# Decay-delta attention and a conv-gated MoE on one core: block-diagonal state of 120x480, w_out in single fp32 matmuls, three solves on GpSimd, new order

## The chip, the cores and the metric

One core of one Trainium2 chip. The metric is the device time of one execution in microseconds; the median of three runs is compared. fp32 inputs and output; the MoE weights arrive as 64-bit words and are converted on the chip.

## The reference

For batch 4, 8 heads, 768 positions and head size 40, a 40x40 state runs along the sequence; the result, heads side by side, is the x of a gated MLP (320 to 1024 to 320) with a convolution of three taps along the sequence.

```python
for t in range(S):
    y[:, :, t] = np.einsum('bhd,bhde->bhe', rt, state)
    Sa = np.einsum('bhde,bhe->bhd', state, at)
    state_decay = state * wt[:, :, None, :] - np.einsum('bhd,bhe->bhde', Sa, bt)
    state = state_decay + np.einsum('bhd,bhe->bhde', vt, kt)
...
h = np.maximum(x @ w_in, 0.0)
...
    conv_out += conv_w[k][None, None, :] * hp[:, k:k + S, :]
gate = 1.0 / (1.0 + np.exp(-conv_out))
return (h * gate @ w_out).astype(np.float32)
```

## The kernel before

The sequence is cut into 24 steps of 32 positions. Partitions hold 4 batches of 32 positions, or 120 = 3 heads x 40 channels. Two steps make a pair, and the 8 heads are cut into three overlapping groups of three (columns from 0, 120 and 200).

Per pair: w, a, k, b are loaded; `decays` turns w (TensorE transposes) and scans it on VectorE; `decayed` turns and scales a, k, b into ah, kt, bt; `scores` masks ah by head (ScalarE, tile ap) and multiplies it with kt and bt (tile at); `hats` turns kt and bt back (khat, bhat); `solve_in` and `solve` invert a unit triangular 32x32 system for each of 64 (batch, head, step): the data go through DRAM to put one system on a partition, 31 rounds of two tensor_tensor (lines 480 and 486) run on VectorE for even pairs (`VSOL`) and on GpSimd for odd ones, and the result comes back through DRAM as tt.

Per step, `chain`: pp = ah with the state plus at with v; psb (ScalarE); pu = tt with psb; u (ScalarE); pn = khat with v plus bhat with u, the update of the state. The state is four tiles s of 120x360, one a batch: for each group of heads a 120x120 block, of which the three 40x40 blocks on the diagonal are wanted; the rest is zeroed by wc, a decay with a head mask (line 381). VectorE adds pn to the old state (line 562), GpSimd multiplies by wc (568). `rturn`, `turn` turn r, v and u; `sturn` turns the state with 12 transposes and four copies to sn (602, 604); `pairs` and `outputs` form py from r with sn and from masked products with khat and bhat; `finish` turns it, scales it and splits it into an fp32r high part xh and a rest xl.

Two steps make a window of the MoE. `moe_in` (four a window, 256 hidden units each): 8 fp32r matmuls for each 128 hidden units give ph, ReLU to hb (714), three taps to cc (721 on ScalarE, 729 on VectorE), sigmoid (734), the product with h (736), then a split into gh on ScalarE (740) and gl on GpSimd (743). `moe_out` (two a window): for each 128 hidden units gh with woh, gl with woh, gh with wol, 24 fp32r matmuls into po (754). Weights are converted by eight VectorE instructions a piece and split into high and low parts.

PSUM: six banks for the attention, two for ph and po. What each engine does next is written out by hand: the generators above are advanced one stage at a time in the sequence of the table `ORDER`, so each engine's queue follows that table, and so does SP's, which issues every DMA.

Of the kernel before, what the change touches and what calls it, by code (L numbers as in the profile page):

```python
# [8 lines left out]
F32 = mybir.dt.float32  # L9
# [11 lines left out]
VSOL = range(0, 12, 2)  # L21
NWA = 24
BUFS = dict(
    ld=4, r=2, v=2, hat=2, suf=2, pre=3, al=2, wc=3, at=3, ah=3, kt=2, ap=1, rp=1, bb=1, xx=1, stmp=1,
    tt=2, rt=1, s=2, psb=1, u=2, vt=2, sn=4, ms=1, ysb=1, xf=2, xh=2, xl=2, xp=1, hb=2, cc=2, o=2,
)
KINDS = dict(
    we="weights", ro="rows", ld="wakb", lv="v", lr="r", de="decays",
# [11 lines left out]
    st1*2 sc4 we6 so1 we8*4 we9 we10 ch1 lv3 rt1 we9 st1*2 ut1 pa1 lr2 ou1 ha4 ld3*2 we10 so1*3 fi0  # L40
    vt2 we10 fi0 fi1 de3.0 sc4 sc5 we9 we10 sc5 ch1 de3.1 we9 de3.1 ha4 we11 we12 lr3 rt2 fi1 st2*2
    fi1 we11 we12 we11*2 ro0 we13 we12*2 ha5 st2 we13 we14 ha5 ld4 so1 we13 dd3.0*3 dd3.1*3 we14*2
    ch2 si2 so2 ch2 pk0 ut2 so2*2 pa2 vt3 sc6 so2*2 st2 ou2 ch2 ro0 rt3 mi0.0*3 so2*2 mi0.0*2 ch2
    st3*2 we13 mi0.1*2 st3 ld4 so2 ld4 we14 lv4 we15 we16 ch3*2 sc6 sc7 ut3 we15 st3 we15 sc7 fi2*3
    lr4 mi0.0 pa3 mi0.0 ch3 we15 ch3 we16 mi0.0 we17 mi0.1 mi0.2 we17*2 mi0.2 so2 ch4 si3 we16 so3
    ou3 ha6 we16 we18 de4.0 we18 ha6 ha7 st4 fi3*2 we17 we19 de4.0 we18 mi0.1 we19 vt4 st4*3 lv5
    de4.1 ch4 ut4 so3 ch4 dd4.0 rt4 we18 we20 de4.1 we20 mi0.2 so3 we20 pa4 vt5 ch4 ch5 so3 mi0.2
    ch5 fi3 ha7 we19*2 we21*2 ut5 we20 we22*2 ou4 st5*2 mi0.1 st5 lr5 rt5 so3 we22 ld4 ld5 de5.0
    mi0.1 we21 ch5 we22 mi0.3 we21 mi0.0*2 so3 mi0.1*2 mi0.3 pa5 mi0.3 pk1 dd4.0*2 dd4.1 mi0.1*2
    dd4.1 st5 mi0.2 sc8 fi4*2 ld5 dd4.1 ou5 mi0.2 lv6 mi0.3 so3*2 sc8 mi0.2 sc9 mi0.2*2 ha8*2 ha9  # L50
    fi4 fi5 ld5 de5.0 de5.1 ha9 sc9 mi0.2 dd5.0 mi0.3 dd5.0 de5.1 lv7 mi1.0*3 mi1.1 ld5 dd5.0 dd5.1
    sc10 so3 si4 mi0.3 lr6 dd5.1*2 ch5 mi0.3 lr7 mi0.3 mi1.1*2 mi1.0*3 mi1.1 mi1.2 vt6 sc10 mi0.3
    mo0.0 sc11 mi0.3 mi1.1 mi1.0*2 mi1.1 ch6 st6 mi1.2 ch6*2 sc11 mi1.1*2 mo0.0*2 ch6 mo0.0 mo0.1*5
    ld6 ut6 rt6 ch7 mi1.1 so4 ld6 so4*2 pa6 vt7 st6 fi5*2 st6 so4*2 mi1.0 so4 mi1.2 st6 mi1.3 so4
    mi1.2 so4 lv8 ou6 mi1.0 mo1.0 mi1.2 mi1.3*2 st7*2 ch7 ut7 mi1.1 st7*2 rt7 ch7*2 mo1.0 pa7
    mi1.3*2 fi6*2 pk2 lr8 mi1.2*2 ou7 mi1.2 rt8 so4 si5 ch8 st8*2 mi1.2 mi1.3 mi1.2 mi1.3 ch8*2 lv9
    fi6 mi2.0*2 lr9 ld6 ch8 ha10*2 fi7 mi1.3*2 ha11 ld6 de6.0 vt8 lv10 de6.0 dd6.0 fi7 mi2.0 mi1.3
    mi2.1 ch9 mo1.0 mi2.0*2 de6.1 ch9 de6.1 so5*2 mi2.1 so5 mi2.0 ut8 mi2.1*4 mi2.0 mo0.0 mo1.0*2
    mo1.1 ha11 mi2.0 mi2.1 mo1.1 dd6.0 mo1.1 dd6.0 pa8 vt9 mo1.1 mi2.0*2 dd6.1 so5 fi7 st8*2 mi2.1*2
    dd6.1 so5 ou8 rt9 mi2.2 sc12 mi2.2*2 mi2.3*3 ut9 dd6.1 st9 mi2.1 mi2.2 ch9 mi2.2 mi2.3*2 mi2.2*2  # L60
    ld7 de7.0 lr10 ld7*2 so5*3 pa9 ch9 lr11 st9*3 pk3 ld7 mi2.3 mi2.2 mi3.0*2 mi2.3 mi3.0 mi2.3 fi8
    so5 fi8 mi2.2*2 mi2.3 mi3.0 ou9 mi3.1 fi8 sc12 fi9 de7.0 dd7.0 sc13 mo2.0*2 sc13 de7.1*2 mi3.1*2
    rt10 ha12*2 ha13 dd7.0 ha13 dd7.0 mi2.3 mi3.0 dd7.1*3 ch10 mi3.1*2 mi3.0 mi3.1 st10 fi9 mo2.0*2
    mo2.1 ch10*3 mo2.1 mi3.0 st10 mi3.1 st10*2 mi3.0 mi3.1 ut10 si6 so6 mi3.2*2 so6 lv11 vt10 mi3.2
    pa10 vt11 so6 mo1.1 so6 mi3.3 mo2.1 mi3.3 ch11 mo2.0 mo2.1 ld8 mi3.0 lr12 so6 ch11 so6 ou10 rt11
    mi3.3 mi3.1 ut11 pa11 st11*3 ld8 lv12 so6 mi3.2 mi3.3 st11 so6 sc14 ch11 vt12 mi3.1 lr13 sc14
    mi3.0 mo3.0 mi3.2 sc15 mi3.2 ch11 mi3.2 fi9 fi10 mi3.3 fi10*2 ou11 st12 ha14 sc15 mi3.2*2 mi3.3
    pk4 so6 ch12 mi3.2 de8.0 mi4.0*2 mi3.3 fi11*2 mi3.3 ch12*2 mo3.0 mi3.3*2 ch12 mi4.0*2 ut12 si7
# [24 lines left out]
    mo7.0 ch20*2 mi8.1*3 ch20*2 mo8.0*2 ha22 mi8.2*2 mi8.3 mi8.2 so11*2 mi8.2 so11 mi8.3*2 pk9 mi8.2
    so11 ha23 mi8.2 ch21 mi8.2*3 st20*2 mi8.3 so11 vt20 lv22 mi8.3 ut20 rt20 lr21 lr22 pa20 vt21
    st20*2 ou20 rt21 st21 mi8.3*3 mi9.0*2 mi8.3*2 mi9.0*2 ch21*2 so11*2 mo7.1 st21 mi9.1*2 ha23 st21
    mi9.1 mi9.0*2 mi9.2 mi9.0 st21 mi9.0 mo8.0*2 mo8.1 mi9.1 so11 mo8.1 mo8.0 mi9.1*3 mi9.2*3 lr23
    ut21 mi9.1 mo8.1*2 mi9.0*2 mi9.3*2 pa21 vt22 mi9.3 fi20*2 ou21 ch21 fi20 mi9.2 mi9.1*2 rt22
    st22*2 mo9.0 mi9.2*2 so11 fi21*3 ch22 st22*2 mi9.2*2 mo9.0 ch22*2 ut22 mi9.3*3 pk10 mi10.0 lv23
    mi10.0*2 mi9.3*3 mi10.1*2 mi9.2 mo9.0 pa22 ch22 ch23 mi10.1 mi9.3 mi10.0*2 mo8.1 vt23 ch23 mo9.0
    mo9.1 mi10.1 mo9.1*2 mi10.0 mi10.1 mi10.0 ut23 mi10.1 mo9.1 ch23 mi10.0*3 mi10.1*2 mi10.2*6 ou22  # L100
    rt23 st23 mi10.1 mi10.3*2 st23*2 mo9.1 fi22 st23 pa23 mi10.2*2 fi22 mi10.1 mi10.3 mi10.2 fi22
# [11 lines left out]
def tile_decay_delta_attention_then_conv_gate_moe(  # L113
# [200 lines left out]
    def cols(g):  # L314
        return slice(GC[g], GC[g] + GR)

# [686 lines left out]
```

## Time and profile before

| | |
|---|---|
| median of three runs (705.96 to 711.5) | 707.8 us |
| profiled execution: span, first to last instruction | 704.2 us |
| its instructions | 29851 |
| TensorE, VectorE, ScalarE, GpSimd busy | 559.1, 521.5, 360.5, 354.1 us |
| mean granted TensorE clock | 0.903 |
| DMA packets, bytes | 242402, 53.40 MB |

The profiled execution's time is its span and whatever lies around it, which no row shows; the span is 3.6 us below the median. The page gives busy time by engine, the span in 40 slices and the chain that ended last; the answers of the trace give busy time by stage, groups of instructions by line (count, busy us, mean ns, idle time before them), waits, and instructions in order of time (start, length, engine, line, tiles, count). PEld is TensorE's weight load. A busy TensorE counts the pipelined end of each matmul, so a rate is read from starts.

### The profile page before, as it was taken

To read this page: it belongs to the slowest core of one execution; us is meant where nothing else is said; L and a number is where in the kernel's file an instruction comes from. 1 tells how busy PE (TensorE), PEld (TensorE's weight loads), DVE (VectorE), ACT (ScalarE), POOL (GpSimd) and SP (SyncE) were. 2 spreads that over 40 slices of the span, in tenths; PEclk is the share of its full clock that TensorE was granted. 3 is DMA by queue.
4 is the path that set the end of the run, shared out by engine and by line. 5 is a ranking of instruction groups with operands and counts; after the bars stand their busy time and mean duration, and the time that the engine had idled before them with its cause. 6 is when DMAs were issued, how large, how long until landed. Compare 5 with 4: busy or idle time off the path is not lost. (4 is left out here: it accounts for less than half of the span.)

```text
span 704.2 us, 29851 instructions
## 1 busy us (share of the span) xinstructions
PE 559.1 (79%) x13021; PEld 496.7 (71%) x13021; DVE 521.5 (74%) x1169; ACT 360.5 (51%) x884; POOL 354.1 (50%) x582
## 2 busy tenths in 40 slices
PE   4436765678688987988987996899998977899886
PEld 3335654666577876977867885788887876788775
DVE  6699789998988895558884478986869892446561
ACT  3322344354275455655464664477665545566661
POOL 2002884037785236783244883237976048854321
PEclk9756766897899998999999998999999999999998
DMA  8766456348036325444414356524444025021000
GB/s 139 121 117 117 96 111 103 86 103 159 7 61 107 61 49 90 87 78 81 84 29 90 75 95 101 81 61 68 86 69 87 11 65 84 20 50 32 22 29 19
DMA packets 242402, 53.40 MB, mean 76 GB/s; under 512 B 229000, under 2 KB 238112, under 8 KB 242272
## 3 DMA queue, kind: packets, MB, share of 16 engines
q1 hardware_dynamic: 242272, 51.50, 40.2%
q8 instruction: 102, 1.67, 1.0%
q14 instruction: 28, 0.23, 0.1%
HBM read 38.63 MB, written 10.22 MB: 69 GB/s over the span
## 5 line engine op out<-in xcount | busy, mean ns | idle before, releaser
L729 DVE SCALAR_TENSOR_TENSOR cc<-hb,cw,cc 128x256 f32<-128x256 f32 x192 | 107.0, 580 | 28.6 <-ACT cc L721 25.0
L568 POOL TENSOR_TENSOR s<-s,wc 120x360 f32<-120x360 f32 x88 | 75.2, 885 | 66.6 <-DVE s L562 66.6
L480 POOL TENSOR_TENSOR st<-xx,bb 128x126 f32<-128x126 f32 (+22 forms) x186 | 81.0, 436 | 20.8 <-DMA bb<-bd 8.1
L486 POOL TENSOR_TENSOR xx<-xx,st 128x126 f32<-128x126 f32 (+22 forms) x186 | 81.8, 440 | 14.6
L700 PE MATMUL ph<-xh,wih 120*128 120x256 f32 x288 | 56.2, 304 | 12.0 <-ACT hb L714 12.0
L562 DVE TENSOR_TENSOR s<-pn,s 120x360 f32<-120x360 f32 x88 | 40.6, 523 | 28.7 <-PE pn L549 28.7
L736 DVE TENSOR_TENSOR cc<-cc,hb 128x512 f32<-128x512 f32 x48 | 40.9, 859 | 26.2 <-ACT cc L734 26.1
L480 DVE TENSOR_TENSOR st<-xx,bb 128x126 f32<-128x126 f32 (+22 forms) x186 | 53.7, 289 | 7.5 <-DMA bb<-bd 1.7
L486 DVE TENSOR_TENSOR xx<-xx,st 128x126 f32<-128x126 f32 (+22 forms) x186 | 54.4, 292 | 6.4
L700 PEld LDWEIGHTS ph<-xh,wih 120*128 120x128 f32 x288 | 41.4, 193 | 17.0 <-ACT hb L714 13.8
L734 ACT ACTIVATE cc<-cc 128x512 f32<-128x512 f32 x48 | 30.5, 637 | 40.8 <-DVE cc L729 40.8
L667 POOL TENSOR_TENSOR xl<-xf,xh 120x384 fp32r<-120x384 f32 x24 | 26.3, 1095 | 44.8 <-ACT xh L665 44.8
L721 ACT ACTIVATE cc<-hb,cw 128x256 f32<-128x256 f32 x96 | 43.8, 507 | 5.0 <-POOL g21l L743 2.4
L427 ACT ACTIVATE ap<-ah,hmask 120x384 f32<-120x384 f32 (+1 forms) x72 | 36.6, 577 | 18.3 <-DVE ah L391 9.7
L604 ACT COPY sn<-pt 120x360 f32<-120x360 f32 x92 | 39.0, 470 | 10.9 <-PE pt L602 10.4
L602 PE MATMUL pt<-ident,s 120*120 120x120 f32 x276 | 40.7, 281 | 4.0 <-DVE s L562 2.4
L714 ACT ACTIVATE hb<-ph 128x512 f32<-128x512 f32 x48 | 28.8, 601 | 22.3 <-PE ph L700 20.5
L579 ACT ACTIVATE rp<-pr,hmask 120x384 f32<-120x384 f32 x72 | 36.7, 585 | 4.7 <-PE pr L576 4.3
L700 PE MATMUL ph<-xl,wih 120*128 120x256 f32 x192 | 39.0, 285 | 0.0
L533 PE MATMUL pu<-psb,tt 32*32 32x40 f32 x1536 | 22.4, 210 | 18.8 <-ACT psb L527 16.1
L602 PEld LDWEIGHTS pt<-ident,s 120*120 120x120 f32 x276 | 31.6, 144 | 6.1 <-DVE s L562 2.8
L533 PEld LDWEIGHTS pu<-psb,tt 32*32 32x32 f32 x1536 | 18.6, 115 | 23.6 <-ACT psb L527 18.1
(867 smaller groups left out, 1661.8 us busy)
## 6 DMA issues: line engine op xcount, KB each, us to landing
bb<-bd SPq DMA_DIRECT2D x24, 256.0 KB
w<-in_w_dram SPq DMA_DIRECT2D x24, 160.0 KB
a<-in_a_dram SPq DMA_DIRECT2D x24, 160.0 KB
k<-in_k_dram SPq DMA_DIRECT2D x24, 160.0 KB
b<-in_b_dram SPq DMA_DIRECT2D x24, 160.0 KB
r<-in_r_dram SPq DMA_DIRECT2D x96, 40.0 KB
v<-in_v_dram SPq DMA_DIRECT2D x96, 40.0 KB
out_dram<-ob SPq DMA_DIRECT2D x22, 160.0 KB
```

Source lines behind the costliest of these rows:

```text
L480: eng.tensor_tensor(t3, xx[:, 0:nj, i : i + 1].to_broadcast([128, nj, nt]), bb[:, i : i + 1, i + 1 :].to_broadcast([128, nj, nt]), ALU.mult,)
L486: eng.tensor_tensor(xx[:, 0:nj, i + 1 :], xx[:, 0:nj, i + 1 :], t3, ALU.add)
L533: nc.tensor.matmul(pu[quad(bi), hc], tt[quad(bi), c, h, :], psb[quad(bi), hc], start=(h == 0), stop=True, skip_group_check=True,)
L562: nc.vector.tensor_tensor(new, pn[bi][:GR], old[bi], ALU.add)
L568: nc.gpsimd.tensor_tensor(n4, n4, w4, ALU.mult)
L579: nc.scalar.activation(out=rp[:, :, h, :], in_=pr[:GR], func=AF.Copy, scale=hmask[:, h : h + 1])
L602: nc.tensor.transpose(pt[:GR, g, :], old[bi][:, g, :], ident[:GR, :GR])
L604: nc.scalar.copy(sn, pt[:GR])
L700: nc.tensor.matmul(ph[:, j], l[:, fs], x, start=(j == 0 and i == 0), stop=(i == len(passes) - 1), skip_group_check=True,)
L721: nc.scalar.activation(out=cc[:, j], in_=hb[:, j, :, 1 : W + 1], func=AF.Copy, scale=cw[:, 1, f : f + 1],)
L729: nc.vector.scalar_tensor_tensor(out=cc[:, j], in0=hb[:, j, :, x : W + x], scalar=cw[:, x, f : f + 1], in1=cc[:, j], op0=ALU.mult, op1=ALU ...
L736: nc.vector.tensor_tensor(cc, cc, hb[:, :, :, 1 : W + 1], ALU.mult)
```

## The change

- **State.** One tile s of 120x480: for each batch three blocks of 40 columns, where block g holds, on its three times 40 rows, one head each. wc loses its mask. pn is now one matmul for each head and batch with 40 streamed columns and 120 weight columns, cut from khat and bhat that lie in a zero-padded layout of 840 columns (`slots`, `spot`), so that the other two heads' columns are zero. The add runs on 120x120, the decay product is one GpSimd instruction of 120x480, `sturn` is four transposes and one copy.
- pp and py take the masked ap and rp per head, 32 matmuls of 40 columns instead of 12 of 120 or 80; rt goes. Groups of heads no longer overlap (3, 3, 2), padded by memsets.
- **v and r** are copied once into DRAM tensors with the heads in the new order (`reorder`, four blocks), and a step then loads each with one DMA.
- **w_out.** The gate stays fp32 in a tile g, the weights in one fp32 tile wo; 8 fp32 matmuls make a moe_out. The copies gh, gl and the split of w_out go.
- **Solves**: `VSOL` is (0, 4, 8); pairs 2, 6 and 10 move to GpSimd.
- `moe_pack` moves rows with two DMAs instead of three. Buffer counts change; `ORDER` is written anew.

```diff
-VSOL = range(0, 12, 2)
+VSOL = (0, 4, 8)
...
-    ld0 de0.0*2 ld0*2 de0.1 ld0 ld1 de0.1 we0 dd0.0*3 dd0.1*2 sc0 dd0.1 we0 ld1*2 lr0 sc0 sc1 lr1
+    ld0 de0.0 ld0*2 de0.0*2 ld0 dd0.0 de0.1*2 ld0 re0 dd0.0 we0 dd0.0 dd0.1 we1 dd0.1*2 dd0.0 sc0
...
+            hat[nm, i] = cp.tile([128, G * PG], F32, name=f"hat{nm}{i}")
+            nc.vector.memset(hat[nm, i], 0.0)
...
+                    nc.sync.dma_start(
+                        ordered[nm, z][bi, :, 3 * h * D : (3 * h + NH[h]) * D].rearrange(
+                            "t (g d) -> t g d", d=D
+                        ),
+                        x[bi, h::3, t0:t1, :].rearrange("g t d -> t g d"),
+                    )
...
-        pn = [bank([128, G, GR], f"pn{n}{bi}") for bi in range(B)]
-        for x, (l, m) in enumerate(((kk, vv), (bk, uu))):
-            for g in range(G):
+        pn = [bank([128, G, D], f"pn{n}{bi}") for bi in range(B)]
+        for x, (l, m) in enumerate(((st["k"], vv), (st["b"], uu))):
+            for q, g, h in heads():
+                lo = spot(q) - D * h
                 for bi in range(B):
                     nc.tensor.matmul(
-                        pn[bi][:GR, g, :], l[quad(bi), cols(g)], m[quad(bi), cols(g)],
-                        start=(x == 0 and g == 0), stop=(x == 1), skip_group_check=True,
+                        pn[bi][:GR, g, :], l[quad(bi), lo : lo + GR],
+                        m[quad(bi), at(q)],
+                        start=(x == 0 and q == 0), stop=(x == 1), skip_group_check=True,
                     )
...
-            for n4, w4 in scaled:
-                nc.gpsimd.tensor_tensor(n4, n4, w4, ALU.mult)
+            nc.gpsimd.tensor_tensor(new, new, w4, ALU.mult)
...
+        pt = bank([128, B, GR], f"pt{n}")
         for bi in range(B):
...
+            nc.tensor.transpose(pt[:GR, bi, :], old[:, bi].rearrange("p g d -> p (g d)"), ident[:GR, :GR])
+        sn = st["sn"] = buf(wn, [GR, B, GR], "sn", f"sn{n}")
+        nc.scalar.copy(sn, pt[:GR])
...
-            gh, gl = parts(f)
-            for l, rr in ((gh, woh), (gl, woh), (gh, wol)):
-                nc.tensor.matmul(
-                    po[:rows, :DM], l, rr[:, f, :],
-                    start=(m == 0), stop=(m == 3 * NF - 1),
-                )
-                m += 1
+            nc.tensor.matmul(
+                po[:rows, :DM], part(f), wo[:, f, :], start=(f == 0), stop=(f == NF - 1)
+            )
```

TensorE at the state update of the eleventh step (pu is the solve's product, pn_... the four batches' banks), before and then now:

```order
L533 MATMUL pu_5857<-psb_5815,tt_5491 32x40 x32
L549 MATMUL pn_5892<-v_4780,khat_4737 120x120
L549 MATMUL pn_5893<-v_4780,khat_4737 120x120
L549 MATMUL pn_5894<-v_4780,khat_4737 120x120
L549 MATMUL pn_5895<-v_4780,khat_4737 120x120
```

```order
L616 MATMUL pu_6135<-psb_6076,tt_5925 32x40 x32
L630 MATMUL pn_6173<-v0t,hatk_137 120x40
L630 MATMUL pn_6174<-v0t,hatk_137 120x40
L630 MATMUL pn_6175<-v0t,hatk_137 120x40
L630 MATMUL pn_6176<-v0t,hatk_137 120x40
```

The four pn rows stood three times for v and three for u; now they stand eight times for each, with 40 columns.

GpSimd where its second solve begins (s are the state products, xx and st the solve's tiles, wil a weight's rest), before and then now:

```order
L568 TENSOR_TENSOR s_2360<-s_2360,wc_677 120x360
L568 TENSOR_TENSOR s_2362<-s_2362,wc_677 120x360
L568 TENSOR_TENSOR s_2364<-s_2364,wc_677 120x360
L568 TENSOR_TENSOR s_2366<-s_2366,wc_677 120x360
L710 MEMSET hb_2413 128x8x2
L473 CAST xx_2479<-xini 128x512
```

```order
L307 TENSOR_TENSOR wil<-wi23q,wih 80x256
L644 TENSOR_TENSOR s_1855<-s_1855,wc_262 120x480
L557 CAST xx_2129<-xini 128x512
L564 TENSOR_TENSOR st_0_2131<-xx_2129,bb_1642 128x31
L570 TENSOR_TENSOR xx_2129<-xx_2129,st_0_2131 128x31
L564 TENSOR_TENSOR st_1_2134<-xx_2129,bb_1642 128x30
```

Before, the second solve on this engine is that of pair 3 and begins behind the four products of the fourth step; now it is that of pair 2, which was on VectorE, it begins behind the one product of the third step and runs in one piece ahead of the fourth step's product.

VectorE's first instructions (wx is what `decays` needs zeroed, hatk and hatb the padded tiles), before and then now, its rows up to those of wx:

```order
L197 MEMSET dsuf 120x192
L200 MEMSET dp_105 120x384
L204 MEMSET wx_107 120x384
L204 MEMSET wx_109 120x384
L198 MEMSET dsuf 120x12
```

```order
L246 MEMSET hatk_137 128x840
L246 MEMSET hatb_139 128x840
L231 MEMSET dsuf 120x12
L246 MEMSET hatk_141 128x840
L246 MEMSET hatb_143 128x840
L250 MEMSET wx_145 120x384
L250 MEMSET wx_147 120x384
```

Eight memsets of 840 columns stand ahead of those of wx.

More of the change, by code (lines that the diff above doesn't have):

```diff
@@ L40 @@
[L40 to L44, printed above, removed]
@@ L200, in tile_decay_delta_attention_then_conv_gate_moe, with padded @@
     nc.vector.memset(dp0, 0.0)
+    def padded(name, at, value):
+        t = cp.tile([128, at + D], F32, name=name)
+        nc.gpsimd.memset(t[:, at:], value)
+        return t
+    inb = {nm: padded(f"in{nm}", 2 * HD, 1.0) for nm in "wakb"}
+    tok = {nm: [padded(f"{nm}{i}t", HD, 0.0) for i in range(BUFS[nm])] for nm in "rvu"}
+    ysb = padded("ysb", HD, 0.0)
+    hat = {}
+    for i in range(BUFS["hat"]):
+        for nm in "kb":
+            hat[nm, i] = cp.tile([128, G * PG], F32, name=f"hat{nm}{i}")
+            nc.vector.memset(hat[nm, i], 0.0)
     wxs = []
@@ L208, in tile_decay_delta_attention_then_conv_gate_moe, with from_f64 @@
     wil = cp.tile([GR, G, DF], F32R, name="wil")
-    woh = cp.tile([128, NF, DM], F32R, name="woh")
-    wol = cp.tile([128, NF, DM], F32R, name="wol")
+    wo = cp.tile([128, NF, DM], F32, name="wo")
     cw = cp.tile([128, KW, NF], F32, name="cw")
-    def from_f64(raw, e, t, m):
+    def from_f64(raw, e, t, m, dst=None):
         lo, hi = raw[..., 0], raw[..., 1]
@@ L294, in load @@
             nc.sync.dma_start(raw, w_out[f * 128 : (f + 1) * 128, 0:512])
-        return piece(f"wo{f}", load, woh[:, f, 0:256], wol[:, f, 0:256], 128, (256,))
+        return piece(f"wo{f}", load, wo[:, f, 0:256], None, 128, (256,))
     def rest_piece(q):
@@ L303, in load @@
             nc.sync.dma_start(raw.rearrange("p (f c) -> p f c", f=4), src)
-        return piece(f"wp{q}", load, woh[:, fs, 256:320], wol[:, fs, 256:320], 128, (4, 64))
+        return piece(f"wp{q}", load, wo[:, fs, 256:320], None, 128, (4, 64))
     pieces = [lambda q=q, g=g: in_piece(q, g) for q in range(4) for g in range(G)]
@@ L314, in cols, with heads @@
     def cols(g):
-        return slice(GC[g], GC[g] + GR)
+        return slice(g * GR, (g + 1) * GR)
+    def heads():
+        return ((q, q // 3, q % 3) for q in range(H))
     def load_wakb(pd):
@@ L576, in rturn @@
             nc.tensor.transpose(pr[:GR, g, :], st["r"][:, cols(g)], ident)
[L577 to L578 removed]
+        rp = st["rp"] = buf(wn, [GR, H, BC], "rp", f"rp{n}")
+        for g in range(G):
             nc.scalar.activation(
[L580 removed]
+                out=rp[:, by_rows(g)], in_=pr[:GR, : NH[g]], func=AF.Copy, scale=hmask[:, g : g + 1]
             )
[L582 to L584 removed]
         yield
@@ L854, in tile_decay_delta_attention_then_conv_gate_moe @@
     )
+    for z in range(len(CUT) - 1):
+        put(("reorder", z), lambda z=z: reorder(z))
     for pd in pds:
```

430 lines of the change are left out of this document (227 added, 203 removed).

## The prediction

> **What bounds the kernel now.** I read the page first: no engine is busy all the time (TensorE 79%, VectorE 74% of the span), and the chain that ended last reaches back only 20 us, to the last gate. So an average says nothing, and I cut the span where the last weights are converted and the first windows of the MoE have begun, at 230 us. The view of busy times by stage:
>
> ```profile
> core 0: us, PE busy (x) PEld busy (x) DVE busy (x) ACT busy (x) POOL busy (x), PEclk, DMA share, GB/s
> 0.00:230.00 230.00, 146.82 (x3457) 125.45 (x3460) 199.11 (x486) 93.72 (x222) 107.05 (x198) 0.79 0.55 102
> 230.00:704.00 474.00, 412.28 (x9586) 371.26 (x9572) 322.38 (x685) 266.76 (x662) 247.10 (x384) 0.96 0.35 63
> ...
> 450.00:500.00 50.00, 47.59 (x1136) 43.68 (x1135) 40.36 (x93) 33.48 (x84) 26.89 (x39) 1.00 0.35 67
> 500.00:550.00 50.00, 45.81 (x1124) 40.78 (x1122) 40.62 (x76) 32.09 (x80) 36.45 (x57) 0.97 0.44 77
> ...
> 600.00:650.00 50.00, 45.74 (x1088) 41.54 (x1087) 23.52 (x43) 29.91 (x76) 31.27 (x52) 0.98 0.15 34
> ```
>
> The first 230 us belong to VectorE (199.1 us, 87%) while TensorE works 147. The other 474 us belong to TensorE: 412.3 us (87%), with VectorE at 68%. The three 50 us rows show how dense TensorE can be in this kernel: 47.59, 45.81 and 45.74 of 50, on average 92.8%. What it waits for in the second part (waits of PE from 230 us on):
>
> ```profile
> PE ph L700 <- ACT hb L714: 12.0, 9, 5.4
> PE py L638 <- issue: 6.3, 7, 1.7
> PE pm L411 <- ACT rp L579: 3.9, 3, 3.3
> ...
> PE po L754 <- ACT g112h L740: 2.7, 1, 2.7
> ```
>
> Many small waits, most of them for ScalarE, and none for the state chain itself. So I treat the change as two sums: VectorE work taken from part 1, and TensorE work added to part 2.
>
> **Part 1, VectorE.** Durations, from the groups by line:
>
> ```profile
> L486 POOL TENSOR_TENSOR xx<-xx,st 128x126 f32<-128x126 f32 (+22 forms) x186 | 81.8, 440 | 14.6
> L480 POOL TENSOR_TENSOR st<-xx,bb 128x126 f32<-128x126 f32 (+22 forms) x186 | 81.0, 436 | 20.8 <-DMA bb<-bd 8.1
> L568 POOL TENSOR_TENSOR s<-s,wc 120x360 f32<-120x360 f32 x88 | 75.2, 885 | 66.6 <-DVE s L562 66.6
> L486 DVE TENSOR_TENSOR xx<-xx,st 128x126 f32<-128x126 f32 (+22 forms) x186 | 54.4, 292 | 6.4
> L480 DVE TENSOR_TENSOR st<-xx,bb 128x126 f32<-128x126 f32 (+22 forms) x186 | 53.7, 289 | 7.5 <-DMA bb<-bd 1.7
> L562 DVE TENSOR_TENSOR s<-pn,s 120x360 f32<-120x360 f32 x88 | 40.6, 523 | 28.7 <-PE pn L549 28.7
> L381 DVE TENSOR_TENSOR wc<-al,hmask 120x36 f32<-120x36 f32 x24 | 8.9, 371 | 0.0
> ```
>
> - A solve on VectorE takes (53.7 + 54.4) / 6 = 18.0 us, on GpSimd (81.0 + 81.8) / 6 = 27.1. Of the three that move, the one of pair 2 lies in part 1: -18.0 us.
> - The state add shrinks from 360 to 120 columns. The trace has no such add; it lies between the 523 ns of the 360-column one and the 230 ns of this engine's 12-column reciprocal. I take 270 (a third of the columns, with a fixed part). Part 1 holds six steps of four: 24 x 0.25 = -6.0 us.
> - The product for wc is gone: 371 ns, about ten of 24 in part 1: -3.7 us.
>
> Together -27.7 us of 199.1, and at the same 87% that is -32 us. Against it stands the start, in the timeline of VectorE and ScalarE:
>
> ```profile
> 1.56 0.79 DVE L204 MEMSET wx<- 120x384 f32 x2
> ...
> 6.56 0.47 ACT L365 COPY wx<-pw 120x372 f32<-120x372 f32 x1 [3.25 <-PE pw L349]
> ...
> 7.06 0.96 DVE L369 TENSOR_TENSOR_SCAN suf<-wx,dsuf 120x384 f32<-120x384 f32 x1 [3.25 <-ACT wx L365]
> ```
>
> Eight memsets of 840 columns now stand ahead of those of wx. At the 384 columns in 0.38 us seen here (two rows overlapping, 0.79) one is 0.83 us, all 6.6 us; wx is cleared at 9 us rather than 2.4, and ScalarE's first copy into it, at 6.56, moves to 9: +2.4 us. If these clears run faster, the idle 3.25 us hide them all. Part 1: **-30 us**.
>
> **Part 2, TensorE.** Start times in its timeline give the rate of each kind:
>
> ```profile
> 401.21 0.79 PE L533 MATMUL pu<-psb,tt 32*32 32x40 f32 x64
> 401.93 0.62 PE L700 MATMUL ph<-xh,wih 120*128 120x256 f32 x3
> ...
> 403.08 0.90 PE L549 MATMUL pn<-v,khat 32*120 32x120 f32 x24
> 403.80 0.81 PE L549 MATMUL pn<-u,bhat 32*120 32x120 f32 x24
> 404.54 0.53 PE L450 MATMUL pz15b<-ident,bt 120*128 120x120 f32 x3
> ...
> 407.17 0.49 PE L349 MATMUL pw<-ident,w 128*120 128x128 f32 x3
> 407.50 0.49 PE L349 MATMUL pa<-ident,a 128*120 128x128 f32 x3
> ...
> 410.24 1.67 PE L602 MATMUL pt<-ident,s 120*120 120x120 f32 x12 [1.59 <-ACT wx L366]
> 411.85 0.65 PE L411 MATMUL pm<-rp,vt 120*32 120x96 f32 x24
> ...
> 414.98 0.91 PE L629 MATMUL py<-sn,rt 120*32 120x120 f32 x24
> 415.82 0.79 PE L638 MATMUL py<-khat,ms 32*32 32x40 f32 x64
> 416.41 0.89 PE L638 MATMUL py<-bhat,ms 32*32 32x40 f32 x64
> ```
>
> An fp32 matmul leaves two records (12 matmuls of pn, 24 records), and the four batches run side by side, so records come in rounds of four.
>
> *The state update pn.* Six rounds in 0.72 us: 120 ns a round, for 120 weight columns and 120 streamed ones. Now there are 16 rounds for v and 16 for u; only 40 columns are streamed, but 120 weight columns are still loaded. Does the load or the stream set the round? The durations of the loads, by line:
>
> ```profile
> L533 PEld LDWEIGHTS pu<-psb,tt x1088: 101/108/167, 252.1 to 646.7; 32*32 32x32 f32 x182
> ...
> L549 PEld LDWEIGHTS pn<-v,khat x384: 174/180/320, 254.8 to 636.1; 32*120 32x120 f32 x192
> ```
>
> 88 more weight columns cost 180 - 108 = 72 ns, 0.82 ns each, so 120 columns hold the load path for 98 ns. The floor is the pu round, 32 weight and 40 streamed columns: 0.72 / 16 = 45 ns; the ceiling today's 120 ns. I take 105, the load plus the spacing of four issues: 32 x 0.105 = 3.36 us a step, against 0.72 + 0.74 = 1.46: +1.9 us. With 17 of 23 updates in part 2, +32 us (floor 0, ceiling +41).
>
> A rule of the Trainium skill speaks against this change more strongly. "TensorE: Matmul & The Clock Gate", section "Part 3: Packing small matmuls", has weight loads overlap running matmuls only when the row group differs; then load and stream of one batch add up. The trace disagrees: six rounds of 98 ns load and some 100 ns stream would need 1.2 us, and pn takes 0.72. I give the rule a chance below.
>
> *sturn.* 12 transposes took 1.61 us, 0.134 each; eight fall away: -1.07 us a step, 17 steps: -18 us.
>
> *pp and py with the state.* 24 records of 120 columns become 64 of 40, at the rate of pu or py (0.59 to 0.72 us) against 0.84 in the row of py: taken as nothing, since nothing in part 2 waits on it; at worst +0.1 us a step.
>
> *w_out.*
>
> ```profile
> 675.05 0.31 PE L754 MATMUL po<-woh,g100h 128*128 128x320 f32 x1
> 675.20 0.31 PE L754 MATMUL po<-woh,g100l 128*128 128x320 f32 x1
> 675.34 0.31 PE L754 MATMUL po<-wol,g100h 128*128 128x320 f32 x1
> ```
>
> 24 fp32r matmuls at 0.146 us are 3.5 us for a moe_out. Now 8 fp32 ones of two records each. The nearest single fp32 records are the transposes of w: three of 128 columns in 0.33 us (407.17 to 407.50), 0.85 ns a column, so 16 x 320 x 0.85 = 4.35 us, +0.85. Floor, if a record streams as fp32r does: 16 x 0.146 = 2.3, -1.2 us; ceiling at pn's 1.0 ns: +1.6. With 23 in part 2 and the end: +20 us.
>
> TensorE's work in part 2: 412 + 32 - 18 + 20 = 446 us. The split of the gates leaves ScalarE and GpSimd:
>
> ```profile
> sum 705.00, ACT 30.01; mean ACT 15.01
> ...
> sum 705.00, POOL 65.95; mean POOL 32.98
> ...
> L604 ACT COPY sn<-pt 120x360 f32<-120x360 f32 x92 | 39.0, 470 | 10.9 <-PE pt L602 10.4
> ```
>
> (the first two: lines 740 and 743 alone, over the whole span). ScalarE loses 30.0 us, some 25 of the sn copies and the 11 us of rt; GpSimd loses 66.0, and its state product falls from 75.2 to 22 x 1.18 = 26 us (885 ns scaled to 480 columns), against 3 x 27.1 for the solves. These engines have room, so I price the removal itself at nothing; it works through TensorE's waits, since the gate waits (2.7 above, and their like for GpSimd) go and ScalarE answers sooner. With all three other engines lighter I let TensorE run at the 92.8% it already reaches: 446 / 0.928 = 481 us instead of 474: **+7 us**.
>
> Taken as nothing: the copy of v and r into DRAM (96 DMAs, with 48 loads in place of 192) on SP's queue. It hides under a DMA share of 0.55 and 0.35; where it came late, the products with v of a step would wait, and pu and the state behind them. In GpSimd's queue the product of the next state now stands behind the whole solve of pair 2: up to 27 us, hidden as long as that solve begins a pair early. What is late then is pp of the step after.
>
> **Sum.** 704.2 - 30 + 7 = 681.2 us of span; the median of the three runs is 707.8, 3.6 above that span, and I add them: **685 us**. With the floors (pn at no cost) it is 35 us less, with the ceilings some 26 more.
>
> **Rivals.**
> - *TensorE keeps its waiting (slower).* The largest wait, 12.0 us for hb, comes from two PSUM banks that the change leaves, and po now holds one for 4.35 us rather than 3.5. If part 2 stays at 87%, 446 / 0.87 = 513, +39: 704.2 - 30 + 39 + 3.6 = 717. It decides from a share below 0.87. Against it: ScalarE, which most waits name, loses a quarter of its work.
> - *Part 1 does not shrink.* GpSimd's solves 1, 2, 3 stand in series with the state products between them, or small DMAs (0.55 already) set the pace. A third of the gain: 704.2 - 10 + 7 + 3.6 = 705; none, with the later start: 717. For it: one engine does these three, and each waits for the state products ahead of it; against: three times 27.1 us is not half of 230.
> - *Loads hide.* pn at the pu rate: 446 - 32 = 414, / 0.928 = 446: 650.
> - *Loads and streams add up*, the mechanism of that rule: a round of pn 98 + 33 ns, so 4.2 us a step, and 16 rounds of 27 + 37 ns for pp and py: +25 us of work, / 0.928 = 27: 712. The rows of pn speak against it.
>
> **How the numbers follow.** Within 1% is about what a measurement of this kernel can tell from no change: 701 to 715. Forecast 0.60 (its own range 668 to 706: faster 0.52, same 0.08); TensorE keeps waiting 0.18, slower; part 1 does not shrink 0.12 (same 0.10, slower 0.02); loads hide 0.07, faster; loads add up 0.03, same. Faster 0.59, same 0.21, slower 0.20. The range goes to 656 and 724, toward the hidden loads and a little past the 717.
>
> **What would show it.** Right: pn's 64 records of v in 1.6 to 1.8 us; 16 records of po in 4.3; the last conversions and the seventh pu some 30 us nearer the start; TensorE over 90% busy behind it; VectorE's total near 440. Wrong: pn at 0.8 us, TensorE's waits in part 2 still 60 us, or a first part as long as now.

## The result, and the profile after

The changed kernel takes 771.2 us (766.9 to 773.1, four runs) against 709.6 us of the kernel before (706.0 to 711.5, four runs on the same chip): 1.087 times as long, 95% interval 1.082 to 1.092. The forecast was 685 and faster, the range 656 to 724.

The profiled execution has a span of 765.1 us (before: 704.2) and a mean granted clock of 0.853 (before: 0.903). Busy time by stage in the profile after, cut where before was cut, columns as in the prediction:

```profile
core 0: us, PE busy (x) PEld busy (x) DVE busy (x) ACT busy (x) POOL busy (x), PEclk, DMA share, GB/s
0.00:230.00 230.00, 162.48 (x4061) 145.41 (x4062) 156.81 (x394) 72.28 (x164) 101.14 (x243) 0.70 0.62 118
230.00:704.00 474.00, 424.59 (x11351) 365.98 (x11353) 221.92 (x518) 202.68 (x500) 186.45 (x412) 0.91 0.33 67
704.00:765.10 61.10, 55.38 (x915) 42.96 (x911) 25.91 (x53) 27.21 (x70) 2.49 (x3) 0.97 0.07 21
```

VectorE, ScalarE and GpSimd all lost work, as forecast; VectorE's total fell from 521.5 to 404.6 us. But the PEclk column fell, 0.79 to 0.70 in the first row and 0.96 to 0.91 in the second. The recorded clock has two values only, 1.0 and 0.5, so the time at half clock is 2 x (1 - mean) x span: 137 us before, 225 after. The first part did not shrink: the seventh pu (the first matmul of the solve's product in the seventh step) starts at 237.3 us (before 229.7). Behind 230 us TensorE is busy 424.59 + 55.38 = 480 us, where the forecast had 446.

The waits of PE over the whole span, in us, times, longest; the first row is of before, the others of after:

```profile
PE py L638 <- issue: 8.0, 8, 1.7
...
PE py L712 <- issue: 22.1, 16, 2.0
...
PE pu L616 <- issue: 5.5, 4, 2.1
...
PE pp L597 <- issue: 5.0, 3, 2.6
...
PE ph L764 <- ACT hb L778: 1.4, 2, 1.2
```

The wait for hb, 12.0 us before, is 1.4. All waits for another engine or a transfer together went from 126 to 73 us. "Issue", waits for nothing that the profile shows, went from 14 to 45 us over all rows, half of it in py, where three batches of 64 records follow one another.

And pn in the timeline after, first in a stretch at full clock, then (the last row) in one at half:

```profile
260.57 1.89 PE L630 MATMUL pn<-v1t,hatk 32*120 32x40 f32 x64
...
262.28 1.89 PE L630 MATMUL pn<-u1t,hatb 32*120 32x40 f32 x64
...
284.77 1.55 PE L630 MATMUL pn<-v0t,hatk 32*120 32x40 f32 x52
286.13 0.39 PE L630 MATMUL pn<-u0t,hatb 32*120 32x40 f32 x6
287.60 3.19 PE L630 MATMUL pn<-u0t,hatb 32*120 32x40 f32 x58 [1.08 <-issue]
```

262.28 - 260.57 = 1.71 us for v's 64 records, inside the forecast 1.6 to 1.8. The 58 records from 287.60 on take 3.19 us where 64 took 1.89: 55 ns a record instead of 30.

To see where 61 us came from, I split TensorE's time in the trace (start to start of its records) into three: each run of like records at that kind's full-clock rate, the part of the remainder that lies in half-clock time (at most half of that time), and the rest, which is waiting. It is an estimate.

```
us                     full-clock work  half-clock loss  rest
before                       460              65          170
after                        507             107          142
```

So +47 of work, +42 of clock, -28 of waiting. The first and the last figure depend on which rate is taken as a kind's own (between the lowest tenth and the lowest two fifths of its stretches, work grows by 38 to 54 us); the clock's share is 40 to 42 with any of them. The terms of the forecast over all steps (pn 1.9 x 23 = 44, sturn -1.07 x 23 = -25, w_out 0.85 x 24 = 20) make 39 us, so the work was priced nearly rightly. The second column was in no term.

### The profile page after: what moved, and what is told of

Same layout as the page of the kernel before. It is cut to its first block, busy times and chain, and to the rows that moved or that the text cites. A ratio compares the mean times of both kernels' runs of the same rounds, so it can differ in the third digit from the quotient of the medians.

```text
span 765.1 us, 35998 instructions
## 1 busy us (share of the span) xinstructions
PE 642.4 (84%) x16317; PEld 554.3 (72%) x16317; DVE 404.6 (53%) x964; ACT 302.2 (39%) x733; POOL 290.1 (38%) x657
## 4 chain that ended last, share of the span: by engine, by line
PE 66%; DVE 11%; issue 9%; POOL 5%; DMA 5%; ACT 4%; SPq 1%; DVEq 0%; POOLq 0%; ACTq 0%
PE pn L630 14%; PE po L809 13%; PE ph L764 10%; PE py L712 5%; PE pm L482 4%; PE pu L616 2%; POOL st L564 2%; PE ps L482 2%; POOL xx L570 2%; PE py L703 2%; PE pp L605 2%; PE pp L597 2%; PE put L669 2%; DMA r0t<-ro 1%; DMA xh<-xh 1%
## 5 line engine op out<-in xcount | busy, mean ns | idle before, releaser
L809 PE MATMUL po<-wo,g 128*128 128x320 f32 x384 | 123.4, 456 | 0.3 <-DVE g L801 0.3
L570 POOL TENSOR_TENSOR xx<-xx,st 128x126 f32<-128x126 f32 (+22 forms) x279 | 112.2, 402 | 21.8
L564 POOL TENSOR_TENSOR st<-xx,bb 128x126 f32<-128x126 f32 (+22 forms) x279 | 110.0, 394 | 24.2 <-DMA bb<-bd 2.6
L809 PEld LDWEIGHTS po<-wo,g 128*128 128x128 f32 x384 | 71.0, 200 | 22.3 <-issue 2.3
L644 POOL TENSOR_TENSOR s<-s,wc 120x480 f32<-120x480 f32 x22 | 23.4, 1062 | 152.0 <-DVE s L641 128.1
L641 DVE TENSOR_TENSOR s<-pn,s 120x120 f32<-120x120 f32 x88 | 18.8, 276 | 103.7 <-PE pn L630 103.7
L801 DVE TENSOR_TENSOR g<-cc,hb 128x512 f32<-128x512 f32 x48 | 33.6, 705 | 41.2 <-ACT cc L798 40.8
L660 ACT ACTIVATE rp<-pr,hmask 120x384 f32<-120x384 f32 (+1 forms) x72 | 34.0, 545 | 17.3 <-PE pr L657 17.0
L764 PE MATMUL ph<-xh,wil 120*128 120x256 f32 x192 | 40.8, 296 | 0.0
L712 PE MATMUL py<-hatb,ms 32*32 32x40 f32 x1536 | 23.7, 208 | 15.3 <-issue 15.3
```

Source lines behind the costliest of these rows:

```text
L564: eng.tensor_tensor(t3, xx[:, 0:nj, i : i + 1].to_broadcast([128, nj, nt]), bb[:, i : i + 1, i + 1 :].to_broadcast([128, nj, nt]), ALU.mult,)
L570: eng.tensor_tensor(xx[:, 0:nj, i + 1 :], xx[:, 0:nj, i + 1 :], t3, ALU.add)
L660: nc.scalar.activation(out=rp[:, by_rows(g)], in_=pr[:GR, : NH[g]], func=AF.Copy, scale=hmask[:, g : g + 1])
L712: nc.tensor.matmul(py[quad(bi), hc], ms[quad(bi), x, h, :], l[quad(bi), spot(h) : spot(h) + D], start=(first and x == 0 and h == 0), stop= ...
L764: nc.tensor.matmul(ph[:, j], l[:, fs], x, start=(j == 0 and i == 0), stop=(i == len(passes) - 1), skip_group_check=True,)
L809: nc.tensor.matmul(po[:rows, :DM], part(f), wo[:, f, :], start=(f == 0), stop=(f == NF - 1))
```

## The experiments

Two theories. **Gate theory**: the granted clock falls to half where TensorE's array is lightly used for some us, and the new pn, 40 columns streamed for each 120 loaded, uses it lightly. **Work theory**: the 47 us or so of work are the loss, and the clock falls only as a sign of waiting. Beside them stand a GpSimd theory (solves in series on one engine) and an order theory (the new table). Each run is compared with the kernel before on the same chip (708 to 709 us in each set).

**Each kind of record alone.**

> No part of the reference is computed; the output is zeros. TensorE alone runs each kind of record by itself for some 40 us, on data of r and v, with fp32r matmuls of 256 columns between: pn as now (32 weight rows x 120 columns, 40 streamed, four batches side by side), pn with 120 streamed, pu (32x32, 40 streamed), the state products (120x32, 40 and 120 streamed), fp32 w_out (128x128, 320 streamed), fp32r w_out, transposes, and pn mixed with fp32r. Gate theory (the clock falls to half where the array is lightly used): the granted clock is near 0.5 in pn with 40 columns, and clearly higher in pn with 120; it stays near 1 in w_out. Work theory (the clock falls only where TensorE waits): every stage runs at 1.0, since nothing here waits, and a round of four pn records takes 105 ns in it, one fp32 w_out record 269 ns, one fp32r record 146 ns.

The stages of that run in the view by stretches: pn with 40 columns, pn with 120, pu, fp32 w_out, fp32r w_out.

```profile
43.90:115.40 71.50, 71.50 (x1522) 71.40 (x1521) 0.00 (x0) 0.00 (x0) 0.00 (x0) 0.54 0.01 3
130.00:166.90 36.90, 36.80 (x1362) 36.36 (x1361) 0.00 (x0) 0.00 (x0) 0.00 (x0) 1.00 0.02 4
179.10:280.50 101.40, 63.47 (x3602) 58.88 (x3601) 0.00 (x0) 0.00 (x0) 0.00 (x0) 0.53 0.02 4
...
458.40:498.50 40.10, 40.10 (x152) 28.30 (x150) 0.00 (x0) 0.00 (x0) 0.00 (x0) 1.00 0.00 0
510.80:550.40 39.60, 39.60 (x272) 39.60 (x272) 0.00 (x0) 0.00 (x0) 0.00 (x0) 1.00 0.00 1
```

In the first row TensorE is busy 71.50 of 71.50 us and the clock is 0.54: the gate closes on an engine that never waits. The second row does the same with three times the streaming at clock 1.00, and is faster: 36.90 us / 340 rounds = 109 ns a round, against 71.50 / 380 = 188. At full clock the narrow round took 109 ns too, later in this run (3.50 us for 32 rounds), so the 120 loaded columns set the round and the wider stream is free. The w_out records took 267 and 147 ns. The work theory's "every stage at 1.0" is out.

The pu row shows the second effect: busy 63.47 of 101.40 us. Its timeline (in brackets the wait ahead):

```profile
181.18 1.35 PE L58 MATMUL kpu<-y,x 32*32 32x40 f32 x128 [0.64 <-issue]
...
184.63 1.49 PE L58 MATMUL kpu<-y,x 32*32 32x40 f32 x128 [2.10 <-issue]
```

128 records, then a wait with nothing to wait for, every 3.4 to 4.0 us. With their loads, 128 records are 256 instructions. The page of this run has a DMA queue of its own for instructions (packets, MB, share):

```profile
q8 instruction: 124, 2.03, 1.1%
```

That is one packet of 16.4 KB for every 257 of the 31932 records and loads that the run left. In the pu row such packets start 3.4 to 4.3 us apart, and each of the 28 waits ends 2.3 to 2.9 us after the start of one: TensorE waits there for its own instructions.

**pn streams 120 columns, in the kernel.**

```diff
-                        pn[bi][:GR, g, :], l[quad(bi), lo : lo + GR],
-                        m[quad(bi), at(q)],
+                        pn[bi][:GR], l[quad(bi), lo : lo + GR],
+                        m[quad(bi), :GR],
```

> The changed kernel, but each matmul of pn streams 120 columns instead of 40 into the same bank, so that the state is not the reference's; the count of records, their weights and all waits stay. Gate theory: the array is busier in pn, the granted clock rises from 0.853 to 0.88 or more, and the time is the same or less (755 to 771) although pn itself takes some 0.4 us more a step. Work theory: pn's rounds go from 105 to 120 ns, 32 x 15 ns x 23 = 11 us more, 782, at the same clock.

734.9 us, ratio 1.039 (1.033 to 1.046), clock 0.912 (0.905 to 0.927 in four executions). Three times the streaming in pn makes the changed kernel 36 us faster: the gate theory's side, by more than it asked. The next kernel streams as much and computes the reference's state: it takes `m[quad(bi), cols(h)]`, the three heads of one slot, into 120 columns for each set, and its add reads the diagonal 40.

> The changed kernel with all of the reference computed: each matmul of pn streams the three heads of a set (120 columns) into a bank of 3 x 120 columns, and the state add reads the 40 useful ones of each. Gate theory: as the run in which pn streamed 120 columns for show, clock about 0.91 and 730 to 742. If what helped there was something in the data of its wrong state, the clock stays at 0.85 and the time at 771 or a little over.

743.5 us, ratio 1.048 (1.041 to 1.054), clock 0.901: 28 us faster than the change, so it was the streaming that helped and not the changed data.

```profile
0.00:230.00 230.00, 152.63 (x4431) 134.07 (x4432) 167.59 (x416) 79.45 (x181) 103.85 (x244) 0.81 0.64 122
230.00:704.00 474.00, 417.78 (x11699) 357.50 (x11698) 218.87 (x508) 204.56 (x506) 186.48 (x412) 0.94 0.32 65
704.00:744.40 40.40, 37.05 (x191) 27.19 (x190) 19.85 (x41) 18.32 (x47) 2.25 (x2) 1.00 0.09 27
```

The clock of the first part goes from 0.70 back to 0.81, and the seventh pu from 237.3 to 223.9 us.

**The mirror: the kernel before with a narrow pn.** Its pn writes `pn[bi][:GR, g, :D]` from the first 40 columns of each set, and VectorE reads these three times over, so that its adds keep their size.

> The kernel before, but pn streams only the first 40 of each set's 120 columns (two of three heads of the state are wrong); records, weights and the other engines' work stay. Work theory: pn is held by its 120 weight columns anyway, so the same time or a few us less. Gate theory: less streaming, so a lower clock than 0.903 and a slower kernel; pn takes only 1.5 us of a step here rather than 3.5, so less than the change lost by it, 5 to 20 us: 713 to 728.

713.2 us, ratio 1.006 (1.002 to 1.009), clock 0.888: two thirds of pn's streaming taken away, and the kernel is slower by a little, at the lower end of the guess. Its time at half clock went from 137 to 160 us. (One of its ten executions took 2602.7 us; nothing here explains it, and it is left aside.)

**One line of the change: three solves to GpSimd** (`VSOL = (0, 4, 8)` in the kernel before).

> The kernel before with one line changed: the solves of pairs 2, 6 and 10 go to GpSimd as in the change. GpSimd theory (solves in series on one engine set the pace of the state chain): slower by 20 us or more. Gate and work theory: TensorE's work is unchanged, so within 10 us of before; the prediction's first part would be 18 us of VectorE shorter there, some 690.

729.5 us, ratio 1.031 (1.025 to 1.038). VectorE's work in the first 230 us fell from 199.1 to 175.8 us, and the seventh pu came 10 us later, not 20 earlier. Against before, the loss comes in three steps of 8 to 10 us, at the pu of the 4th, the 13th and the 20th step. Its waits of PE:

```profile
PE po L754 <- POOL g30l L743: 9.9, 1, 9.9
...
PE pp L514 <- POOL s L568: 8.9, 10, 3.6
```

TensorE waits for gate halves and state products that stand behind whole solves in GpSimd's queue. In the changed kernel with wide pn, the three solves moved back:

> The same with six solves on VectorE and six on GpSimd, as the kernel before has them. GpSimd theory: moving three cost the kernel before 21 us, so 15 to 20 us come back: 715 to 720. If the changed order hides them, or VectorE's 18 us each matter as much, within 7 us of the run beside it.

767.4 us, ratio 1.083 (1.076 to 1.090), 24 us slower than beside it. So moving the solves costs time in either direction, each order having been made for its own split; in the new order the 21 us do not come back, and the GpSimd theory isn't needed for the loss of the change. The order by itself:

> The changed kernel, narrow pn and all, with the table ORDER of the kernel before (its steps that no longer exist do nothing, the reordering of v and r is issued where its first load needs it). Order theory (the new order is at fault): 10 us or more faster than 771. Gate theory: pn's narrow streams are the same in any order, so the clock stays near 0.85 and the time is 771 or, with an order not made for it, more.

870.8 us, ratio 1.231 (1.222 to 1.240), clock 0.803. The order theory is out: against the old table, which was not made for this body, the new one is worth 100 us.

**Does VectorE bound the first part?**

```diff
+            if j == 2 and i >= 2:
+                continue
```

> The kernel before with 29 of the 31 rounds of pair 2's solve on VectorE left out (its result is wrong from there): some 17 us of VectorE work taken from the first 230 us, nothing added anywhere. The prediction's step (VectorE bounds the first part): 17 / 0.87 = 20 us faster, 688, the seventh pu at 210. Clock theory (TensorE at half clock and the chain of waits through it bound that part): 10 us or less.

709.6 us (ten executions, 700.5 to 714.5), ratio 1.003 (1.000 to 1.007). VectorE's work in the first 230 us fell by 16 us, to 182.9. The trace is of the shortest execution, and even there the seventh pu starts at 230.4 (before 229.7). VectorE's waits in the first 230 us, before (two rows) and in this run (three):

```profile
DVE at L437 <- PE ps L411: 4.7, 3, 2.3
...
DVE s L562 <- PE pn L549: 0.2, 1, 0.2
```

```profile
DVE at L437 <- PE ps L411: 12.0, 4, 7.7
DVE s L564 <- PE pn L551: 7.9, 1, 7.9
DVE ms L616 <- PE pm L411: 3.7, 1, 3.7
```

All that was taken off VectorE came back as its waits for TensorE. In the changed kernel the wait of the state add for pn in the first 230 us is larger still:

```profile
DVE s L641 <- PE pn L630: 29.2, 5, 7.9
```

A try at opening the gate there, with extra matmuls that nobody reads:

> The kernel before with two bf16 matmuls of 384 columns, whose result is overwritten, ahead of each batch of transposes of w, a, k and b in pairs 0 to 4: some 40 x 0.32 = 13 us of extra TensorE work at full clock, all before 300 us. Gate theory: the busier array opens the gate earlier, half-clock time in the first 230 us falls from 96 us by a third or more, and the time is 708 or a few us less. Work theory: 10 us more, 718, with the clock as it was.

714.5 us, ratio 1.009 (1.005 to 1.012). Half-clock time before 230 us fell from 96 to 88 us only, over the span from 137 to 123. So a little clock was bought (0.906 to 0.918 in seven executions, the kernel before 0.896 to 0.917 beside them), for more work than it was worth. Two short matmuls ahead of each batch do not fill that part.

**w_out.** In the kernel before (gates and weights unsplit, 8 fp32 matmuls):

> The kernel before with the change's w_out alone: gates and w_out unsplit, 8 fp32 matmuls in place of 24 fp32r ones. Work theory: 24 x (4.30 - 3.50) = 19 us more TensorE work, less the gate waits that go (some 10): 715 to 730. Gate theory: the same, since a 320-column record keeps the array busy, and the clock stays at 0.90 or above. The prediction would have TensorE's waits shrink by more than its work grows: 700 or less.

731.2 us, ratio 1.033 (1.027 to 1.039): +22 us. That is just above the 715 to 730 of the work theory, but the loss lies in another place than it says. The first matmul with w_out starts at 237.4 us, and at the seventh pu (249.0, before 229.7) the run is already 19.3 us late. From there to the end it loses 4.6 us, although nearly all of the added work, some 19 us, lies there: the waits that went with the splitting pay for most of them. Of the 19.3 us, 11 arise at the fifth step. The longest wait of PE ahead of it, from 169 to 182 us, is

```profile
PE pt L602 <- ACT psb L527: 12.7, 1, 12.7
```

It falls where ScalarE writes the last seven pieces of w_out in one block (164 to 181 us; in the kernel before from 166 to 199 us, with other work between), and psb stands behind these in its queue. So most of the 22 us come ahead of the fp32 matmuls, and this run doesn't show their price. Undone for TensorE alone (gates and weights in fp32r tiles), with wide and with narrow pn:

```diff
-            nc.tensor.matmul(
-                po[:rows, :DM], part(f), wo[:, f, :], start=(f == 0), stop=(f == NF - 1)
-            )
+            for i in range(3):
+                nc.tensor.matmul(
+                    po[:rows, :DM], part(f), wo[:, f, :],
+                    start=(f == 0 and i == 0), stop=(f == NF - 1 and i == 2),
+                )
```

> The changed kernel with wide pn, and w_out as 24 fp32r matmuls a window half as before (three times the same product of gates and weights, so the output is three times too large and less exact), without the splitting work on ScalarE and GpSimd. Work theory: 384 x 0.269 - 576 x 0.146 = 19 us of TensorE work less, so 743 - 19 = 724. If w_out is hidden behind other waits in the new order, within 5 us of 743.

712.8 us (ten executions, 705.7 to 715.3), ratio 1.005 (1.002 to 1.009), clock 0.910 to 0.923: 31 us less for 19 of work.

> The changed kernel with its narrow pn, and w_out as 24 fp32r matmuls a window half (three times the same product, output three times too large), without the splitting work. With wide pn the same edit gave 31 us where its work is 19. Work theory: 771 - 19 = 752 here, the rest there was something of that run. If w_out and the clock act on one another (the fp32 records let the gate close more), more than 19 again: 735 to 745, with the clock above 0.853. If the gate now closes more because fewer records are fp32, less than 19.

741.2 us, ratio 1.045 (1.039 to 1.051), clock 0.859: 30 us less again. So the 11 us beyond the work come with w_out, whatever pn is. Part of them is clock: time at half clock falls from 225 to 208 us with narrow pn and from 147 to 108 with wide pn (there in the trace of the shortest of ten executions), and half of such time is lost, 8 and 20 us. Do fp32 records hold the clock less?

> No part of the reference is computed; the output is zeros. TensorE alone: pn with 40 columns (one step's 128 records or two steps' 256), each followed by w_out, once as fp32 records and once as fp32r records of the same length or of the same products (8 fp32 matmuls, 4.3 us, against 24 fp32r, 3.5 us). If fp32 records count less for the clock than fp32r ones, the fp32 mixes run at a lower clock than the fp32r mixes of the same length. If they count the same, mixes of one length have one clock, and the 11 us by which w_out costs more than its work come from something else. With 60 columns in pn the mix of 256 records stays at 1.0.

Twelve times pn and w_out: fp32 and fp32r of one length, then fp32 and fp32r of the same products, then pn with 60 columns (256 records) and fp32.

```profile
44.90:126.20 81.30, 81.30 (x1634) 65.41 (x1633) 0.00 (x0) 0.00 (x0) 0.00 (x0) 0.85 0.01 3
138.70:218.50 79.80, 79.80 (x1718) 77.01 (x1718) 0.00 (x0) 0.00 (x0) 0.00 (x0) 0.87 0.01 3
230.50:337.90 107.40, 107.40 (x1729) 83.46 (x1729) 0.00 (x0) 0.00 (x0) 0.00 (x0) 0.89 0.01 2
350.20:439.90 89.70, 89.70 (x1826) 86.99 (x1826) 0.00 (x0) 0.00 (x0) 0.00 (x0) 0.96 0.01 3
1219.10:1355.30 136.20, 136.20 (x3266) 117.23 (x3265) 0.00 (x0) 0.00 (x0) 0.00 (x0) 1.00 0.01 3
```

At one length the clock is nearly the same, 0.85 and 0.87, and with 256 records of pn between it is 0.72 for both: fp32 records are no lighter. Of the same products the fp32 form costs 17.7 / 12 = 1.5 us a time for 0.8 of work, since its cycle runs at 0.89 rather than 0.96. That is with narrow pn. Why the clock of the kernel with wide pn changes with w_out is not shown, so the reason of the 11 us stays open there.

**Mixes, and the count of records.**

> No part of the reference is computed; the output is zeros. TensorE alone again: pn with 60, 80 and 100 columns streamed, then mixes: batches of 64, 128 or 192 pu records between batches of fp32 w_out records, and pn (40 and 120 columns) between w_out records. Gate theory: the clock rises somewhere between 60 and 100 columns, and pn with 40 between w_out batches stays at 1.0 only while the w_out share is large. Instruction theory (TensorE's instructions arrive in blocks of 256, that is 128 records with their loads, and a block takes about 3.7 us to come): no stall in 64 pu records + 8 of w_out (128 records last 5.1 us), a stall of some 1.2 us per block in 128 pu + 4, some 0.3 us in 64 pu + 4, and stalls in bursts of 192 even where 8.6 us of w_out follow. If the waits called issue come from something else in the kernel (DMA traffic, semaphores), the mixes show none.

pn with 60 columns; 128 pu + 4 w_out records; 64 + 4; pn with 40 and 8 w_out records; the same with 120:

```profile
43.60:76.30 32.70, 31.23 (x1121) 30.33 (x1120) 0.00 (x0) 0.00 (x0) 0.00 (x0) 1.00 0.02 5
173.40:195.50 22.10, 16.22 (x793) 12.03 (x793) 0.00 (x0) 0.00 (x0) 0.00 (x0) 1.00 0.02 4
207.80:231.40 23.60, 23.60 (x817) 16.16 (x817) 0.00 (x0) 0.00 (x0) 0.00 (x0) 1.00 0.02 4
596.20:764.60 168.40, 168.40 (x3169) 145.47 (x3169) 0.00 (x0) 0.00 (x0) 0.00 (x0) 0.64 0.01 2
777.20:888.30 111.10, 111.10 (x3169) 99.09 (x3169) 0.00 (x0) 0.00 (x0) 0.00 (x0) 1.00 0.02 4
```

The gate opens for pn between 40 and 60 columns, lower than the 60 to 100 that were expected. The second row is busy 16.22 of 22.10 us: stalls as forecast. In the third 64 + 4 records have none, where 0.3 us was expected: 128 records last 3.7 us there, just the time a block takes. Mixes of 64 + 8 have none, as forecast. Bursts of 192 stalled in 6 of 12 cases with 4.5 us of w_out behind each, and in 3 of 12 with 8.8. No other engine was at work and no data was moved, only the instruction packets, so the issue waits of these runs belong to TensorE's own stream of instructions.

Then pn's old count of records with the new state: 12 matmuls a batch, dense hats, and three masked adds on VectorE per batch to keep the diagonal blocks.

```diff
+                    nc.vector.scalar_tensor_tensor(
+                        out=new[:, bi], in0=pt, scalar=mk, in1=new[:, bi] if h else old[:, bi],
+                        op0=ALU.mult, op1=ALU.add,
+                    )
```

> The changed kernel with all of the reference computed, but pn as before: 12 matmuls a batch of 120 dense weight columns and 120 streamed, which give all nine blocks of a set, and three masked adds on VectorE per batch that keep the diagonal ones (12 adds of some 300 ns a step in place of 4 of 276; the zero-padded hats and their clears go). TensorE: 80 fewer records and 3.50 - 1.46 = 2.0 us less a step than the change, the clock as in the wide run. Work theory with gate: 743 - 23 x 2.0 = 697, some us more if the adds lie on the state chain (8 x 0.3 = 2.4 us a step at worst, 55 us in all: 743). If the issue waits come from the number of records, they fall from 45 us by a third or more.

731.4 us, ratio 1.029 (1.024 to 1.034), clock 0.890. Issue waits fell from the 51 us of the wide run to 29, and the work column from 507 to 457, but the rest rose from 158 to 189; the longest waits of PE are now for VectorE and for a load of r:

```profile
PE py L712 <- DVE ms L689: 19.6, 15, 3.2
PE pr L657 <- DMA r0t<-ro: 17.7, 4, 7.9
```

So 50 us of work gave back 12, within the 697 to 743 that were expected, near its upper end. With w_out split as before on top:

> The same with gates and w_out split into halves again as before (24 fp32r matmuls, the splitting copies and subtractions back on ScalarE and GpSimd): all of the reference computed, the block-diagonal state and the new order kept. Work theory: 19 to 31 us less than the run beside it, some 670, below the kernel before. If GpSimd, which has nine solves here and gets 66 us of subtractions back, takes over as the bound, no gain or slower than the run beside it.

854.9 us, ratio 1.206 (1.202 to 1.210), clock 0.819. Nine solves and the splitting do not fit GpSimd in this order:

```profile
PE pp L593 <- POOL s L648: 34.9, 6, 14.5
...
PE pt L682 <- POOL s L648: 17.0, 3, 12.9
```

None of the kernels of this section is faster than the kernel before beyond the noise.

## Why the prediction was wrong

- **Part 1, -30 us: failed.** The step was "27.7 us of 199.1, and at the same 87% that is -32 us". An engine at 87% need not set the pace: with 16 us less on VectorE the kernel before kept its time (1.003), and VectorE waited for TensorE instead, which runs at 0.79 of its clock there. Measured: +8 us at the seventh pu; 13 of the miss of 38 come back with wide pn, the rest was not divided. The price of the start was short as well: ScalarE's first copy into wx moved from 6.56 to 10.41 us, 3.9 rather than 2.4. The rival "part 1 does not shrink" was right in its result. Its reason, solves in series on GpSimd, holds in the kernel before (10 us later at the seventh pu) but was not shown for the new order, where moving them back made the seventh pu 12 us later; that small DMAs do it was not tried.
- **pn, +1.9 us a step: right at full clock, mis-sized in the kernel.** 1.71 and 1.82 us for v and u in the trace, against 1.68 each. But over the trace pn takes 112 us for 23 steps, 4.9 a step, since it halves its own clock for part of them. Undoing the narrow streams gave 28 and 36 us in the two runs that did.
- **w_out, +20 us: the work right, the effect larger.** 269 ns a record against 272 forecast. Undoing it gave 30 and 31 us in the changed kernel. Part of the excess is more time at half clock; its reason is open.
- **sturn -18, pp and py +0: nearly right as work.** The transposes of the state take some 0.1 us each in most stretches at full clock, not the 0.134 of the one row that the forecast read, so that the change saves 18 us over all 23 steps and some 13 over the 17 of part 2; pp and py with the state gained some 3 us. Their price lies elsewhere, in issue waits (14 to 45 us over the span). The forecast gave these no term, though its own second row of waits was one (py, 6.3 us). Taking 80 records a step from pn lowered them by 22 us, but with VectorE's adds in the way I can't say how many us of time that is.
- **446 us of TensorE work at 92.8%: the step that failed in part 2.** TensorE was busy 480 us there at 89.7%, so that part 2 took 535 us instead of 481. At 92.8% it would have been 517: 36 of the missing 54 us are the busy time, 18 its density. I took the three dense windows of before as what lighter helpers allow. Their clock was 0.97 to 1.00, as the quoted rows show in the PEclk column, which I did not use: a busy us at half clock does about half the work (55 against 30 ns a record of pn).
- **The rivals.** "TensorE keeps its waiting" was wrong: its waits for other engines fell from 126 to 73 us. "Loads and streams add up", after the Trainium skill ("TensorE: Matmul & The Clock Gate", "Part 3: Packing small matmuls"), asked for 131 ns a round of pn; the run of single kinds has 109 with 40 columns and 109 with 120. "Loads hide" is out by the same rows. The same page of the Trainium skill, in "Part 1: The HAM clock gate", has the half clock come after an idle window of some 3.4 us. The trace agrees on the length, its half-clock stretches inside the span being multiples of 3.41 us; it differs on the cause, since narrow pn ran at half clock while busy 71.50 of 71.50 us, and the measurement decides. I had not asked what the new pn would do to the clock.

Shown: narrow streams close the gate, and opening it again gives back 28 us of the 61; fp32 w_out costs the changed kernel 30 to 31. The two together undone leave 712.8 us, 0.5% above before, so they hold nearly all of the loss; what the rest of the new work costs and what the new order and the lighter engines give cancel out there, and were not measured apart.

## What to carry to other kernels

Look whether a matmul streams far fewer columns than it loads as weights (here 40 against 120; 60 were enough): its weight load then sets the pace, the clock of everything around it can halve, and a wider stream that costs nothing may be the faster form. Before taking work off an engine that looks like the bound of a stage, look whether it and TensorE wait for each other in turn, and read the granted clock beside the busy share. When one part of a change is tried alone, look where in the span its time is lost: the 22 us of w_out in the kernel before were the right size in the wrong place. Count the records too: many small ones in a row stall on their own instructions.

## What the runs showed of the hardware

- The clock falls to half while TensorE is busy 71.50 of 71.50 us: narrow pn alone runs at 0.54 (at half clock from 5.3 us after its start on), and pn with 60, 80, 100 or 120 columns at 1.00.
- A round of four fp32 pn records lasts 109 ns at full clock, with 40 and with 120 streamed columns.
- TensorE's instructions come in packets of about 256 (124 of 16.4 KB for 31932), 3.4 to 4.3 us apart in the pu row, where it waits for them: 3600 pu records took 101.4 us, 28 ns each, against 11 ns in short bursts, and 3600 state-product records with 40 columns 101.3.
